# Attention and two feed-forward layers: the first 768 tokens in two phases, with g kept as float32 between the products

## The chip, the cores and the metric

The kernel runs on one core of a Trainium2 chip (trn2). Times are device microseconds of one execution, and the metric is their median over the runs. The engines are TensorE (PE, with its weight loads as PEld), VectorE (DVE), ScalarE (ACT), GpSimd (POOL, unused here) and SyncE (SP), which issues all DMA.

## What is computed

The reference, cut to what matters:

```python
# q, k, v: (4, 8, 576, 64)
scores = (1.0 / np.sqrt(D)) * np.matmul(q, k.transpose(0, 1, 3, 2))
mask = (rel >= 0) & (rel < 64)            # rel: query position minus key position
scores = np.where(mask, scores, -1000000000.0)
attn = softmax(scores)
x = np.matmul(attn, v)                    # heads side by side: (2304, 512)
x = np.maximum(x @ w_in, 0.0) ** 2 @ w_out      # first layer, 512 -> 2048 -> 512
h = x @ w_in2
out = np.maximum(0.01 * h, h) @ w_out2          # second layer
```

Inputs are float32. The host passes the weights as raw 64-bit words, and the kernel makes float32 of them.

## The kernel before

Every matmul of the two layers is done in three products of split operands: a float32 value is a high part (cast to fp32r by ScalarE, line 281) and a low part (the rest, a subtraction on VectorE, line 284), and high x high, high x low and low x high are added in PSUM. A weight chunk of 128 x 512 is first put together from its words: ScalarE scales one word (line 314), VectorE needs three passes (lines 317, 323, 329), and then it is split (lines 281 and 284). There are 16 chunks j of `w_in` and 16 of `w_out`. All 32 are converted once and stay in SBUF.

The 2304 tokens are 18 attention blocks of 128 queries. A block has two halves of four heads. The first four blocks go half by half (`quad`), later ones whole (`duo`): scores on TensorE (line 406) into bank s (and t or h), mask on VectorE (line 375), maximum (427), exponentials on ScalarE (430), sum and reciprocal (436, 437), normalisation (440), transposes (TensorE 463), a copy (ScalarE 281), weighing with the values (TensorE 472), and the split into x (`to_x`, ScalarE 281 and VectorE 284).

The first layer takes the tokens in `BLOCKS` of 512, 384, 512, 384, 512. For each chunk j, `step` computes the first product (line 571, 12 matmuls into a bank h), relu and square on ScalarE, the square again on VectorE (600) for the low part of g, and then the second product (line 617, 12 matmuls), which adds into four banks acc0 to acc3. The order on TensorE is first product of j+1, second product of j. In the first block of 512 tokens the first four chunks are cut into two waves of 256 tokens (`LAG`), since the second 256 tokens' x comes later. The result goes to DRAM as x2.

The second layer's weights are converted into DRAM meanwhile (`weight_to_dram`). The second layer (lines 801 and 890) works on 768 tokens at a time; its second product fills six banks in turn, three matmuls in each.

PSUM has eight banks: acc0 to acc3, two h, s and t. The order of work is not written by hand. Each operation is recorded with an engine, a cost and a due time (`op`), and `Plan.order` places them: a ready operation with the earliest due time goes first on its engine, and buffers are handed out in turn. Each engine then runs its list strictly in that order; SP issues the DMAs in its list in the same way.

Of the kernel before, what the change touches and what calls it, by code (L numbers as in the profile page):

```python
# [34 lines left out]
BLOCKS = [512, 384, 512, 384, 512]  # L35
# [214 lines left out]
def build(ctx, tc, qp, kp, vp, w1, w2, caps, ident, out, prm=PRM):  # L250
# [250 lines left out]
    def quad(i, b, c, e, sp_):  # L501
# [20 lines left out]
    def duo(b, e):  # L522
# [36 lines left out]
    def step(t, i, parts, T, dt, T2, busy, last):  # L559
        x = xt[t]  # L560
        nb = BLOCKS[t]
        hp = slot(ps_h, "h", [P, 512], F32, 2)
        c = slice(parts[0][0], parts[-1][0] + parts[-1][1])
        n = c.stop - c.start
# [3 lines left out]
        def ffn1(c0, n1, j, kk):
            wi = wt[j, 0].ap.rearrange("p v (k f) -> p v k f", k=KD)
            for m, (a, b) in enumerate(((0, 0), (0, 1), (1, 0))):  # L570
                nc.tensor.matmul(  # L571
                    out=hp.ap[:, c0 : c0 + n1], lhsT=wi[:, a, kk, :],
                    rhs=x.ap[:, b, kk, c0 : c0 + n1],
                    start=(kk == 0 and m == 0), stop=(kk == KD - 1 and m == 2),
                )

        for c0, n1, j in parts:
            w = wt[j, 0]
            for kk in range(KD):
                rd = [(x, m, kk, b) for m in range(2) for b in x_cols(t, c0, n1)]  # L580
                op(
                    "pe", 3 * mm_cost(n1), T, lambda a=(c0, n1, j, kk): ffn1(*a),
                    [(w, 0), (w, 1), *rd], [(hp, 0)],
                )
        op("pe", 0.0, T, lambda: None, [(hp, 0)], [("step", t, i)])
        hin = [(hp, 0)]
# [19 lines left out]

        if i == 0:
            acc[t] = [slot(ps_acc, f"acc{d}", [P, nb]) for d in range(KD)]
        ac = acc[t]

        def ffn2(d, ms):
            for m in ms:
                a, b = ((0, 0), (1, 0), (0, 1))[m]
                for c0, n1, j in parts:
                    wo = wt[j, 1].ap
                    begin, end = i == 0 and m == 0, last and m == 2
                    nc.tensor.matmul(  # L617
                        out=ac[d].ap[:, c0 : c0 + n1], lhsT=wo[:, a, d * P : (d + 1) * P],
                        rhs=g.ap[:, b, c0 : c0 + n1], start=begin, stop=end,
                        skip_group_check=True,  # L620
                    )
# [440 lines left out]
```

## Time and profile before

| | |
|---|---|
| median of 3 runs | 871.2 us (870.68 to 872.87) |
| the profiled execution, its own time | 871.45 us |
| its span in the trace | 869.7 us |
| busy: PE, PEld | 849.9 us (98%), 755.1 us (87%) |
| busy: DVE, ACT | 574.8 us (66%), 469.5 us (54%) |
| DMA | 103.59 MB, mean 119 GB/s |

Times inside the trace count from the start of the span. The profiled execution took 1.75 us more than its span, which lies before and after it. A matmul's record includes its way through the array, so the records of neighbours overlap; the distance from one group's start to the next is what a group costs. The same holds for VectorE, where one instruction's end overlaps the next one's start a little. A trace is one execution; the durations here come from it.

### The profile page before, as it was taken

What the parts mean: (1) busy time and instruction counts of PE and PEld (TensorE: products, weight loads), DVE (VectorE), ACT (ScalarE), POOL (GpSimd) and SP (SyncE); (2) the same over time, 40 slices, a digit from 0 to 9 for tenths busy, and PEclk for the clock granted to TensorE, in tenths of its full rate; (3) what the DMA queues carried; (4) which work ended last, traced back from release to release, by engine and by line L of the source; (5) the groups of instructions that cost most, each with busy time, mean ns of one, the idle gap of its engine ahead of it and who ended that gap; (6) DMA issues with size and microseconds to landing.
All of it is one profiled execution on the core that took longest, in us unless ns stands there. A gap on an engine that the chain in (4) does not pass through costs nothing.

```text
span 869.7 us, 13819 instructions
## 1 busy us (share of the span) xinstructions
PE 849.9 (98%) x5224; PEld 755.1 (87%) x5224; DVE 574.8 (66%) x1100; ACT 469.5 (54%) x1079; POOL 0.2 (0%) x4
## 2 busy tenths in 40 slices
PE   7879999999999999999999999999999999999998
PEld 6768887999888879999888899988999888999886
DVE  6989886555665577666768387775487774676530
ACT  4858676445453445444435377753477653667430
POOL 0000000000000000000000000000000000000000
PEclk8989999999999999999999999999999999999999
DMA  7554652223534436433543212431213422223201
GB/s 281 193 206 151 191 197 74 76 86 107 175 119 151 146 103 205 153 117 110 165 142 105 73 49 74 150 116 49 106 65 99 144 73 73 97 73 98 97 0 73
DMA packets 45570, 103.59 MB, mean 119 GB/s; under 512 B 5056, under 2 KB 6336, under 8 KB 45504
## 3 DMA queue, kind: packets, MB, share of 16 engines
q1 hardware_dynamic: 45504, 102.72, 35.2%
q8 instruction: 41, 0.67, 0.3%
q14 instruction: 25, 0.20, 0.1%
HBM read 84.87 MB, written 17.83 MB: 118 GB/s over the span
## 4 chain that ended last, share of the span: by engine, by line
PE 92%; DVE 4%; DMA 2%; ACT 2%; issue 0%; DVEq 0%; SPq 0%
PE acc L617 21%; PE h L571 21%; PE acc L890 15%; PE h L801 9%; PE s L801 6%; PE s L890 4%; PE t L890 4%; PE acc L801 3%; PE t L801 3%; PE t L472 2%; PE s L406 2%; PE t L463 2%; DMA wst<-w2a 1%; PE t L948 1%; DVE e L323 1%; DMA wst<-w1a 1%
## 5 line engine op out<-in xcount | busy, mean ns | idle before, releaser
L617 PE MATMUL acc<-g,w 128*128 128x512 f32 (+2 forms) x1008 | 220.7, 364 | 5.5 <-ACT g L281 4.2
L571 PE MATMUL h<-x,w 128*128 128x512 f32 (+2 forms) x1008 | 219.3, 363 | 3.5 <-DVE w L284 1.9
L617 PEld LDWEIGHTS acc<-g,w 128*128 128x128 f32 x1008 | 178.3, 190 | 27.9 <-ACT g L281 4.5
L571 PEld LDWEIGHTS h<-x,w 128*128 128x128 f32 x1008 | 177.4, 189 | 27.0 <-DVE w L284 2.7
L890 PE MATMUL acc<-w,w 128*128 128x512 f32 x576 | 146.2, 389 | 0.0
L890 PEld LDWEIGHTS acc<-w,w 128*128 128x128 f32 x576 | 108.1, 188 | 22.4
L284 DVE TENSOR_TENSOR w<-wst,w 128x512 fp32r<-128x512 f32 (+1 forms) x144 | 87.3, 642 | 30.0 <-ACT w L281 30.0
L591 ACT ACTIVATE e<-h 128x512 f32<-128x512 f32 (+2 forms) x84 | 45.0, 536 | 113.5 <-PE h L571 111.9
L281 ACT CAST w<-wst 128x512 fp32r<-128x512 f32 (+1 forms) x144 | 78.7, 582 | 44.0 <-PE acc L890 24.7
L801 PE MATMUL h<-w,w 128*128 128x384 f32 x432 | 85.1, 334 | 0.0
L600 DVE TENSOR_TENSOR e<-e 128x384 f32<-128x384 f32 (+1 forms) x64 | 39.9, 623 | 67.7 <-ACT g L599 67.7
L801 PEld LDWEIGHTS h<-w,w 128*128 128x128 f32 x432 | 75.9, 188 | 0.2
L284 DVE TENSOR_TENSOR g<-e,g 128x512 fp32r<-128x512 f32 (+2 forms) x84 | 51.6, 615 | 9.6 <-ACT g L281 4.7
L801 PE MATMUL s<-w,w 128*128 128x384 f32 x288 | 57.9, 335 | 0.0
L314 ACT ACTIVATE wst<-wst 128x512 f32<-128x512 f32 x64 | 42.5, 675 | 20.3 <-DMA wst<-w2b 11.2
L801 PEld LDWEIGHTS s<-w,w 128*128 128x128 f32 x288 | 50.7, 188 | 0.1
L323 DVE SCALAR_TENSOR_TENSOR e<-wst,e 128x512 int32<-128x512 int32 x64 | 44.3, 692 | 1.9
L329 DVE SCALAR_TENSOR_TENSOR e<-wst,e 128x512 int32<-128x512 int32 x64 | 44.2, 690 | 1.7
L640 DVE COPY e<-acc 128x512 f32<-128x512 f32 (+1 forms) x19 | 12.6, 664 | 49.3 <-PE acc L890 27.8
L890 PE MATMUL s<-w,w 128*128 128x512 f32 x144 | 40.5, 389 | 0.0
L890 PE MATMUL t<-w,w 128*128 128x512 f32 x144 | 40.4, 389 | 0.0
L284 DVE TENSOR_TENSOR w<-x,w 128x384 fp32r<-128x384 f32 x54 | 29.5, 553 | 13.9 <-ACT w L281 13.9
(129 smaller groups left out, 1005.5 us busy)
## 6 DMA issues: line engine op xcount, KB each, us to landing
wst<-wf SPq DMA_DIRECT2D x96, 256.0 KB, 2.9
wst<-w1a SPq DMA_DIRECT2D x16, 512.0 KB, 4.3
wst<-w2a SPq DMA_DIRECT2D x16, 512.0 KB, 3.7
v<-vp SPq DMA_DIRECT2D x32, 256.0 KB, 2.9
wst<-w1b SPq DMA_DIRECT2D x16, 512.0 KB, 4.5
wf<-e SPq DMA_DIRECT2D x32, 256.0 KB, 2.2
wst<-w2b SPq DMA_DIRECT2D x16, 512.0 KB, 4.3
w<-x SPq DMA_DIRECT2D x12, 384.0 KB, 4.0
```

The costliest lines, as they stand in the source:

```text
L281: nc.scalar.copy(out=dst, in_=src)
L284: eng.tensor_tensor(out=lo, in0=src, in1=f32(hi), op=ALU.subtract)
L314: nc.scalar.activation(out=top, in_=top, func=AF.Copy, scale=2.0**-112)
L323: nc.vector.scalar_tensor_tensor(out=cv.ap, in0=words(1), scalar=-(1 << 31), in1=cv.ap, op0=ALU.bitwise_and, op1=ALU.bitwise_or,)
L329: nc.vector.scalar_tensor_tensor(out=cv.ap, in0=words(0), scalar=29, in1=cv.ap, op0=ALU.logical_shift_right, op1=ALU.bitwise_or,)
L406: nc.tensor.matmul(out=st.ap[o : o + WIN, h, :], lhsT=q.ap[d, h, o : o + WIN], rhs=k.ap[d, h, o : o + P], start=True, stop=True,)
L571: nc.tensor.matmul(out=hp.ap[:, c0 : c0 + n1], lhsT=wi[:, a, kk, :], rhs=x.ap[:, b, kk, c0 : c0 + n1], start=(kk == 0 and m == 0), stop=(k ...
L591: nc.scalar.activation(out=r.ap, in_=hp.ap[:, c], func=AF.Relu)
L600: op("dve", dve_cost(n), a0 + 1.4, lambda: nc.vector.tensor_tensor(out=r.ap, in0=r.ap, in1=r.ap, op=ALU.mult), [], [(r, 0)])
L617: nc.tensor.matmul(out=ac[d].ap[:, c0 : c0 + n1], lhsT=wo[:, a, d * P : (d + 1) * P], rhs=g.ap[:, b, c0 : c0 + n1], start=begin, stop=end, ...
L801: nc.tensor.matmul(out=ps.ap, lhsT=view(v, i), rhs=xs[s, i][b].ap[:, u], start=begin and i == 0 and m == 0, stop=i == 1 and m == 2, skip_g ...
L890: nc.tensor.matmul(out=accs[3 * h + tt].ap, lhsT=v.ap[:, b, tt * P : (tt + 1) * P], rhs=w.ap[:, a, :], start=n == 0 and m == 0, stop=last ...
```

## The change

`BLOCKS` becomes 512, 256, 512, 512, 512, and the first two, 768 tokens, are done in two phases.

Phase one (`unit`) computes only first products. For chunk j, ScalarE writes relu of bank h as float32 into g and squares it in place; g of all 16 chunks stays in SBUF (16 tiles of 128 x 768: 14 in buffers of the tag w1, two in those of the tag g). The order is given by the list `first`: the first 256 tokens (A) for four chunks, the next 256 (BB) for the same four, all 512 (AB) for chunks 4 to 11, then the last 256 tokens (C) for chunks 0 to 11, then C and AB in turn for chunks 12 to 15. Only `w_in` is needed for that.

Phase two (`out_unit`) computes the second products. For each chunk, ScalarE casts g to its high part, VectorE subtracts for the low part, into one of two buffers `g_split`, which lie where x of the second block was. TensorE then does 12 matmuls of 256 columns (tokens 512 to 767) and 12 of 512 columns. The four accumulators of 512 columns have acc0 to acc3; the four of 256 columns share the two h banks, two in each, and the bank is opened by the first matmul of the first of them alone. The `w_out` chunks are converted for this phase, each into a buffer that an earlier g has left (`gate`).

The later blocks keep the old `step`, always with 512 tokens and without the form with an additional ScalarE pass that the first block had (`busy`). Transposes and weighing of the first six blocks use acc banks. Due times are new, and the second layer's g has one tile more in x1 and none in kl.

```diff
-BLOCKS = [512, 384, 512, 384, 512]
+BLOCKS = [512, 256, 512, 512, 512]
+NFIRST = 2
...
+NG = sum(BLOCKS[:NFIRST])
...
-    def weight(k, c):
+    def weight(k, c, gate=()):
...
-        op("act", act_cost(DM), c + 1.8 * cs, lambda: copy(w.ap[:, 0], f32(cv.ap)), [(cv, 0)], [(w, 0)])
+        op("act", act_cost(DM), c + 1.8 * cs, lambda: copy(w.ap[:, 0], f32(cv.ap)), [(cv, 0), *gate], [(w, 0)])
...
-        if early:
-            tp = slot(ps_acc, f"acc{i % 2 * 2}", [P, HQ, P])
-            pv = slot(ps_acc, f"acc{i % 2 * 2 + 1}", [P, HQ // 2, P])
-        else:
-            tp = slot(ps_t, "t", [P, HQ, P])
-            pv = slot(ps_t, "t", [P, HQ // 2, P])
+        tp = slot(ps_acc, f"acc{i % 2 * 2}", [P, HQ, P])
+        pv = slot(ps_acc, f"acc{i % 2 * 2 + 1}", [P, HQ // 2, P])
...
+    def ffn2(a, w, g, d, ms, first, last):
+        for m in ms:
+            i, b = ((0, 0), (1, 0), (0, 1))[m]
+            nc.tensor.matmul(
+                out=a, lhsT=w.ap[:, i, d * P : (d + 1) * P], rhs=g[:, b],
+                start=first and m == 0, stop=last and m == 2, skip_group_check=True,
+            )
...
+    def unit(t, c0, n, j, T, dt):
+
+        hp = slot(ps_h, "h", [P, n], F32, 2)
+        if j not in first_g:
+            own = (gp, "g", 2) if j >= NCH - 2 else (wp, "w1", NCH)
+            first_g[j] = slot(own[0], own[1], [P, NG], F32, own[2])
+        g = first_g[j]
...
+        ffn1(t, c0, n, j, hp, T)
...
+        op("act", act_cost(n), a0, lambda: nc.scalar.activation(out=part(), in_=hp.ap, func=AF.Relu), [(hp, 0)], keys)
+        op("act", act_cost(n), a0 + 0.7, lambda: nc.scalar.activation(out=part(), in_=part(), func=AF.Square), [], keys)
+
+    def out_unit(m, j, T, accs, gs_):
+
+        g, w, k = first_g[j], wt[j, 1], m % 2
+        for t in (1, 0):
...
+            op("act", act_cost(n), d0, lambda o=o, n=n, part=part: copy(part(0), g.ap[:, o : o + n]), src, [hi])
+            op("dve", dve_cost(n), d0 + 0.7, lambda o=o, n=n, part=part: sub(nc.vector, part(1), g.ap[:, o : o + n], part(0)), [hi, *src], [lo, ("split", m, t)])
+            one = mm_cost(n)
+            for d in range(KD):
+                a = accs[t][d]
+                shared = t == 1 and d % 2 == 1
...
+                    lambda d=d, a=a, o=o, n=n, shared=shared: ffn2(a[1](), w, gs_.ap[:, k, :, o : o + n], d, (0, 1, 2), m == 0 and not shared, m == NCH - 1),
...
+    units(A, range(LA), prm["PA"])
+    t_b = units(BB, range(LA), prm["PB"])
+    units(AB, range(LA, LB), prm["PAB"])
+    t_c = units(C, range(LB), prm["PC"])
+    for j in range(LB, NCH):
+        units(C, [j], 12 * mm_cost(HALF))
+        units(AB, [j], 12 * mm_cost(512))
...
+    g_split = slot(xp, "x1", [P, 2, 2, NG], F32R)
...
+    two = [slot(ps_h, "h", [P, 2, HALF], F32, 2) for _ in range(2)]
...
+    for m, j in enumerate(out_order):
+        weight(2 * j + 1, t_f + m * step1 - prm["LEAD2"], [("split", m - 2, t) for t in range(NFIRST)])
+        out_unit(m, j, t_f + m * step1, acc, g_split)
```

How the change moves instructions, at three places. VectorE in the kernel before, from one low part of x of block 3 to the next, its second half's. Line 317 begins a chunk's conversion, line 284 ends it; w_656 is of `w_in`, w_664 of `w_out`, and x_323 is x of the first 512 tokens:

```order
L284 TENSOR_TENSOR x_323<-t,x_323 128x2x128
L436 TENSOR_SCALAR sm<-sm 128x4
L437 RECIPROCAL rc<-sm 128x4
L440 TENSOR_TENSOR pt<-pt,rc 128x512
L284 TENSOR_TENSOR g<-e,g 128x256
L284 TENSOR_TENSOR w_656<-e,w_656 128x512
L284 TENSOR_TENSOR w_664<-e,w_664 128x512
L317 TENSOR_SCALAR e<-wst 128x512
L323 SCALAR_TENSOR_TENSOR e<-wst,e 128x512
L329 SCALAR_TENSOR_TENSOR e<-wst,e 128x512
L317 TENSOR_SCALAR e<-wst 128x512
L284 TENSOR_TENSOR x_323<-t,x_323 128x2x128
```

VectorE in the changed order, the last rows up to the same low part of x (here x_334; pt and u on lines 378 and 430 are block 4's, and w_591 is the fifth chunk of `w_in`):

```order
L439 TENSOR_SCALAR sm<-sm 128x4
L440 RECIPROCAL rc<-sm 128x4
L443 TENSOR_TENSOR pt<-pt,rc 128x512
L378 SCALAR_TENSOR_TENSOR u<-s,cap 64x512 x2
L430 TENSOR_REDUCE nm<-u 128x4
L287 TENSOR_TENSOR x_334<-acc_306,x_334 128x2x128
L287 TENSOR_TENSOR w_591<-e,w_591 128x512
L320 TENSOR_SCALAR e<-wst 128x512
L326 SCALAR_TENSOR_TENSOR e<-wst,e 128x512
L378 SCALAR_TENSOR_TENSOR pt<-t,cap 64x512 x2
L430 TENSOR_REDUCE nm<-pt 128x4
L287 TENSOR_TENSOR x_334<-acc_318,x_334 128x2x128
```

The low parts of g and the chunks of `w_out` are gone from the list ahead of this x, and block 4's masks and maxima now stand there.

TensorE in the changed order, where the units on the last 256 tokens begin (line 475 weighs block 5, x_334 is x of the first 512 tokens, x_810 of the last 256, w_316 and w_374 are chunks 0 and 1 of `w_in`):

```order
L606 MATMUL h<-x_334,w_910 128x512 x12
L466 MATMUL acc_306<-ident,pt 128x128 x4
L606 MATMUL h<-x_334,w_953 128x512 x9
L475 MATMUL acc_267<-u,v 64x64 x8
L475 MATMUL acc_267<-pt,v 64x64 x8
L606 MATMUL h<-x_334,w_953 128x512 x3
L606 MATMUL h<-x_810,w_316 128x256 x12
L606 MATMUL h<-x_810,w_374 128x256 x12
```

The three matmuls after the weighing are the rest of chunk 11's unit; the next row reads x_810, of which the weighing just made the last block.

TensorE in the kernel before, in the first 512 tokens (w_961 and w_1040 are of `w_in`, w_923 of `w_out`):

```order
L571 MATMUL h<-x_323,w_961 128x512 x12
L617 MATMUL acc_241<-g,w_923 128x512 x2
L617 MATMUL acc_298<-g,w_923 128x512 x2
L617 MATMUL acc_252<-g,w_923 128x512 x2
L617 MATMUL acc_313<-g,w_923 128x512 x2
L617 MATMUL acc_241<-g,w_923 128x512
L617 MATMUL acc_298<-g,w_923 128x512
L617 MATMUL acc_252<-g,w_923 128x512
L617 MATMUL acc_313<-g,w_923 128x512
L571 MATMUL h<-x_323,w_1040 128x512 x12
```

TensorE in the changed order, at the start of phase two (x_1396 is `g_split`, w_1107 the last chunk of `w_in`, w_1161 and w_1179 the first two of `w_out`):

```order
L606 MATMUL h<-x_810,w_1107 128x256 x12
L606 MATMUL h<-x_334,w_1107 128x512 x12
L618 MATMUL h<-x_1396,w_1161 128x256 x6
L618 MATMUL acc_238<-x_1396,w_1161 128x512 x3
L618 MATMUL h<-x_1396,w_1161 128x256 x6
L618 MATMUL acc_306<-x_1396,w_1161 128x512 x3
L618 MATMUL acc_267<-x_1396,w_1161 128x512 x3
L618 MATMUL acc_318<-x_1396,w_1161 128x512 x3
L618 MATMUL h<-x_1396,w_1179 128x256 x12
L618 MATMUL acc_238<-x_1396,w_1179 128x512 x3
```

Where first and second products alternated, all second products of these tokens now follow all first ones, and the h banks hold accumulators.

## Rows read from the trace of the kernel before

**Rows 1.** The page, parts 1 and 2: busy time, and busy tenths in 40 slices.
```profile
PE 849.9 (98%) x5224; PEld 755.1 (87%) x5224; DVE 574.8 (66%) x1100; ACT 469.5 (54%) x1079; POOL 0.2 (0%) x4
...
PE   7879999999999999999999999999999999999998
```

**Rows 2.** Windows: start:end, length, busy of PE, PEld, DVE, ACT, POOL, clock, DMA, GB/s.
```profile
20.00:40.00 20.00, 16.06 (x173) 14.03 (x172) 19.62 (x42) 16.09 (x43) 0.00 (x0) 0.90 0.59 199
40.00:60.00 20.00, 13.51 (x128) 12.06 (x126) 16.68 (x35) 12.90 (x38) 0.00 (x0) 0.83 0.48 170
...
200.00:300.00 100.00, 100.00 (x670) 85.63 (x670) 60.59 (x109) 44.39 (x109) 0.00 (x0) 1.00 0.42 142
553.00:865.00 312.00, 312.00 (x1535) 278.44 (x1534) 192.24 (x383) 169.40 (x338) 0.00 (x0) 1.00 0.25 82
```

**Rows 3.** Critical chain from 60 to 90 us: start us, us, what.
```profile
61.33 2.79 PE h L571 x21
...
67.46 1.44 PE h L571 x12
...
77.27 2.72 PE acc L617 x12
...
84.10 1.13 PE t L472 x32
```

**Rows 4.** VectorE groups by line and form, 0 to 140 us: count | busy us, mean ns.
```profile
L323 DVE SCALAR_TENSOR_TENSOR e<-wst,e 128x512 int32<-128x512 int32 x32 | 22.1, 691 | 0.8
...
L284 DVE TENSOR_TENSOR w<-e,w 128x512 fp32r<-128x512 f32 x31 | 21.0, 686 | 1.8 <-ACT w L281 1.4
L317 DVE TENSOR_SCALAR e<-wst 128x512 int32<-128x512 int32 x32 | 13.5, 421 | 0.4 <-ACT wst L314 0.3
...
L440 DVE TENSOR_TENSOR pt<-pt,rc 128x512 f32<-128x512 f32 x5 | 3.5, 691 | 0.1
...
L427 DVE TENSOR_REDUCE nm<-u 128x4 f32<-128x512 f32 x5 | 3.4, 682 | 0.1
...
L284 DVE TENSOR_TENSOR g<-e,g 128x256 fp32r<-128x256 f32 x8 | 3.4, 419 | 0.0
...
L437 DVE RECIPROCAL rc<-sm 128x4 f32<-128x4 f32 x14 | 2.5, 178 | 0.5
L436 DVE TENSOR_SCALAR sm<-sm 128x4 f32<-128x4 f32 x14 | 2.3, 162 | 0.0
```

**Rows 5.** VectorE in order of time: start us, us, instruction [idle before <-releaser].
```profile
8.06 1.39 DVE L375 SCALAR_TENSOR_TENSOR w<-s,cap 64x512 f32<-64x512 f32 x2 [7.07 <-PE s L406]
...
59.75 0.42 DVE L284 TENSOR_TENSOR x<-t,x 128x256 fp32r<-128x256 f32 x1 [2.21 <-ACT x L281]
```

**Rows 6.** TensorE in order of time: the scores of one block and what follows them.
```profile
309.39 0.33 PE L406 MATMUL s<-kh,qs 64*64 64x128 f32 x2
...
310.42 3.06 PE L571 MATMUL h<-x,w 128*128 128x512 f32 x12
```

**Rows 7.** TensorE groups by line and form, 0 to 61.25 us.
```profile
L571 PE MATMUL h<-x,w 128*128 128x256 f32 x60 | 10.1, 307 | 2.7 <-DVE x L284 1.5 <-DVE w L284 1.1
L617 PE MATMUL acc<-g,w 128*128 128x256 f32 x48 | 9.1, 329 | 5.5 <-ACT g L281 4.2 <-DVE g L284 1.3
```

**Rows 8.** VectorE in order of time: a low part of x.
```profile
86.36 0.69 DVE L284 TENSOR_TENSOR x<-t,x 128x512 fp32r<-128x512 f32 x1
```

**Rows 9.** ScalarE groups by line and form, 0 to 140 us.
```profile
L430 ACT ACTIVATE pt<-pt,nm 128x128 f32<-128x128 f32 x20 | 7.8, 392 | 0.0
...
L281 ACT CAST g<-e 128x256 fp32r<-128x256 f32 x8 | 3.2, 406 | 0.2
...
L430 ACT ACTIVATION_READ_ACCUMULATOR pt<-pt,nm 128x1 f32 x20 | 3.8, 189 | 0.0
```

**Rows 10.** SP's waits, 0 to 150 us: who for whom: total, times, longest.
```profile
SPq L497 <- PE t L472: 34.7, 5, 15.7
```

**Rows 11.** Critical chain from 0 to 140 us.
```profile
44.19 5.45 DMA wst<-w1a
```

More of the change, by code (lines that the diff above doesn't have):

```diff
@@ L557, in x_cols, with step @@
         return range(o // P, (o + n) // P)
-    def step(t, i, parts, T, dt, T2, busy, last):
+    def step(t, j, T, dt, T2, last):
         x = xt[t]
[L561 to L564, printed above, removed]
+        n = BLOCKS[t]
+        hp = slot(ps_h, "h", [P, n], F32, 2)
         r = slot(ep, "e", [P, n])
         g = slot(gp, "g", [P, 2, 512], F32R, 2)
[L568 to L586, printed above, removed]
+        ffn1(t, 0, n, j, hp, T)
+        op("pe", 0.0, T, lambda: None, [(hp, 0)], [("step", t, j)])
         a0 = T + dt + 0.1
@@ L605, in step @@
         )
[L607 to L621, printed above, removed]
@@ L623, in step, with out @@
-        one = sum(mm_cost(p[1]) for p in parts)
-        ws = [wt[p[2], 1] for p in parts]
-        wh, wl = [(w, 0) for w in ws], [(w, 1) for w in ws]
+        if j == 0:
+            acc[t] = [slot(ps_acc, f"acc{d}", [P, n]) for d in range(KD)]
+        w = wt[j, 1]
+        one = mm_cost(n)
+        def out(d, ms):
+            return lambda: ffn2(acc[t][d].ap, w, g.ap[:, :, 0:n], d, ms, j == 0, last)
         if not last:
             for d in range(KD):
-                op("pe", 2 * one, T2, lambda d=d: ffn2(d, (0, 1)), [gh, *wh, *wl], [(ac[d], 0)])
+                op("pe", 2 * one, T2, out(d, (0, 1)), [gh, (w, 0), (w, 1)], [(acc[t][d], 0)])
@@ L960, in build @@
         pair_load(b, e - early - 6.0 if b < prm["NDUO"] else e + gap - prm["DS"] - 6.0)
-    for k in range(2 * NCH):
-        st = next(q for q in steps if q[2][0][2] == k // 2)
-        weight(k, st[3] + (k % 2) * st[4] - prm["LEAD"])
+    for j in range(NCH):
+        weight(2 * j, next(u[4] for u in first if u[3] == j) - prm["LEAD"])
+    new_x(0)
+    new_x(1)
+    g_split = slot(xp, "x1", [P, 2, 2, NG], F32R)
     for i, (e, b, c, gap) in enumerate(quads):
@@ L968, in build @@
             duo(b, e)
-    for n, (t, i, parts, T, dt, wave) in enumerate(steps):
-        last = n + 1 == len(steps) or steps[n + 1][0] != t
-        T2 = steps[n + 1][3] + steps[n + 1][4] if n + 1 < len(steps) else t_end
-        step(t, i, parts, T, dt, T2, wave, last)
+    for n, (t, c0, nb, j, T) in enumerate(first):
+        unit(t, c0, nb, j, T, 12 * mm_cost(nb))
+    accs = {0: [slot(ps_acc, f"acc{d}", [P, 512]) for d in range(KD)]}
+    two = [slot(ps_h, "h", [P, 2, HALF], F32, 2) for _ in range(2)]
@@ new lines, in build, with store @@
+    for t in range(NFIRST):
+        acc[t] = []
+        for d in range(KD):
+            if t == 0:
+                acc[t].append(((accs[0][d], 0), lambda a=accs[0][d]: a.ap))
+            else:
+                acc[t].append(((two[d // 2], d % 2), lambda a=two[d // 2], d=d: a.ap[:, d % 2, :]))
+    for m, j in enumerate(out_order):
+        weight(2 * j + 1, t_f + m * step1 - prm["LEAD2"], [("split", m - 2, t) for t in range(NFIRST)])
+        out_unit(m, j, t_f + m * step1, acc, g_split)
+    def store(t, a, d, due):
+        o, nb = starts[t], BLOCKS[t]
+        evac(a, nb, x2[d][:, o : o + nb], [(("x2", d, t), 0)], d % 2 == 0, due)
@@ L973, in build @@
+    for t in (1, 0):
+        for d in range(KD):
+            store(t, acc[t][d], d, t_start[NFIRST] - 12 * mm_cost(512) * t + prm["EV0"] + prm["EV1"] * (d + 1) / KD)
+    for n, (t, j, T, dt) in enumerate(steps):
+        last = j == NCH - 1
+        T2 = steps[n + 1][2] + steps[n + 1][3] if n + 1 < len(steps) else t_end
+        step(t, j, T, dt, T2, last)
         if last:
-            o, nb = starts[t], BLOCKS[t]
             for d in range(KD):
-                due = T2 + prm["EV0"] + prm["EV1"] * (d + 1) / KD
-                evac(acc[t][d], nb, x2[d][:, o : o + nb], [(("x2", d, t), 0)], d % 2 == 0, due)
+                a = acc[t][d]
+                store(t, ((a, 0), lambda a=a: a.ap), d, T2 + prm["EV0"] + prm["EV1"] * (d + 1) / KD)
```

122 lines of the change are left out of this document (78 added, 44 removed).

## The prediction

> **What bounds the kernel now.** I read the page first, for the slices by engine [rows 1], then the busy time by stretch [rows 2], TensorE's chain in order of time [rows 3], and VectorE's instructions by group [rows 4]. The slices say that TensorE is full almost throughout: 849.9 of 869.7 us, the digits 9 from the fourth slice (65 us) on. So time can be won only before that, or by giving TensorE less work. The stretches say why it isn't full early: VectorE is busy 19.62 of the 20 us from 20 to 40 and 16.68 from 40 to 60, while TensorE is busy 16.06 and 13.51, at a granted clock of 0.90 and 0.83 [rows 2]. A fraction means time at both levels, 1.2 and 2.4 GHz; later stretches have 1.00, all at the upper one.
>
> What ends the poor stretch is one operation: VectorE writes the low part of x for the second half of block 3, the last of the first 512 tokens, from 59.75 to 60.17 us [rows 5]. At 61.33 us TensorE starts first products of the second 256 columns and runs on [rows 3]. Up to there VectorE feeds both products: each chunk of `w_in` and each of `w_out` costs it one L317, one L323, one L329 and one L284.
>
> **The change, term by term.** I work out when that operation comes now, and how much TensorE work is left behind it in each kernel.
>
> *VectorE up to that operation.* In the order of the kernel before there stand up to it 12 L317, 22 of L323 and L329, 10 low parts of weights, 4 of g, 10 masks, 8 maxima, 8 pairs of sum and reciprocal, 8 normalisations and 8 low parts of x. With the means of [rows 4], a mask counted like a normalisation and a low part of x like one of g: 12 x 0.42 + 22 x 0.69 + 10 x 0.69 + 4 x 0.42 + 10 x 0.69 + 8 x 0.68 + 8 x 0.34 + 8 x 0.69 + 8 x 0.42 = 52.7 us. From the first mask at 8.06 us that gives 60.8; the trace has 60.17 [rows 5]. So the method is 0.6 us off: neighbouring instructions overlap a little, and that pays for the waits. In the changed order there stand 6 L317, 11 of L323 and L329, 5 low parts of weights, none of g, 14 masks and 10 maxima (block 4's come earlier), and the same 8, 8 and 8: 2.5 + 7.6 + 3.5 + 9.7 + 6.8 + 2.7 + 5.5 + 3.4 = 41.7 us. From 8.06 us that is **49.7 us**, 11.6 us before the 61.33 at which TensorE ran on. Just ahead on TensorE's queue stand the scores of block 5; the second of their banks comes free with a mask that ends 1.1 us before that operation, at 48.6, and scores take 1.03 us, from 309.39 to 310.42 [rows 6]. So they end at the same time and cost nothing.
>
> *Work left at that point.* Before, 60 first-product and 48 second-product matmuls of 256 columns had run [rows 7]. After, by its order: the same 60, no second-product one, and the scores of block 5 besides those of block 4. Twelve matmuls of 256 columns take 1.44 us, twelve of 512 take 2.72 [rows 3]. So 48 x 0.12 = 5.8 us more is left, less 1.03 for the scores. The whole program has 48 second-product matmuls fewer (960 for 1008, the same columns): two of 256 cost 0.240 us where one of 512 costs 0.227, so this saves 48 x 0.013 = 0.6 us. 5.8 - 1.0 - 0.6 = **4.1 us** more.
>
> *New waits behind it.* The next transposes need a normalisation that stands 1.7 us down VectorE's list, and TensorE asks after 1.44 us: **0.3 us**. The seven chunks of w_in for the units of 512 columns that are not ready yet stand 5.2, 5.9, 10.2, 13.4, 17.3, 21.5 and 23.9 us down that list, by the same means; TensorE asks for them after 7.9, 11.8, 14.5, 17.2, 21.0, 24.1 and 27.3 us. The least cover is 2.6 us; beyond it each late us costs one. Then come twelve units of 256 columns on blocks 4 and 5. They need x of block 5, whose weighing stands only three matmuls of 512 columns (0.7 us) ahead of them. From the end of a weighing (85.23) to the end of such a low part (87.05) is 1.8 us [rows 3, 8]: TensorE waits **1.1 us**.
>
> *Phase two.* TensorE has 16 x (1.44 + 2.72) = 66.6 us, and 11.1 us of attention. VectorE's list (32 low parts of g, 14 of weights, 10 L317, 20 of L323 and L329, three blocks of softmax, four x) comes to 64 us, 82% of that: not the bound. The first split waits for the buffer of x of tokens 512 to 767, free 2.72 us before phase two; ScalarE's cast (0.41) and VectorE's subtraction (0.42) of 256 columns fit [rows 4, 9]. Later splits have more than a unit of 4.16 us. I take 0 for these, and for ScalarE's casts and copies, which run under the same cover. A pair of accumulators in one bank is not in the trace: its matmul is bounded below by the 0.12 us of 256 columns in a bank of their own and above by the 0.227 of 512. It writes 256 columns, so I take 0.12; the upper end would be 192 x 0.107 = 20 us. Transposes that go to the free acc banks add no instruction.
>
> *DMA.* No bytes are added. On SP's queue the `w_out` loads move behind all of `w_in`, and 13 of them ahead of the values of block 7, which can be loaded only after block 6 is weighed. SP stood 15.7 us at one load of values for TensorE's weighing [rows 10]; such waits stay, but only half the weight loads are queued behind them. I take nothing; the cover is the three staging buffers, and if it goes, the chunk's conversion is late and eats the 2.6 us above.
>
> *Later blocks of 512.* TensorE's columns are the same, and VectorE is busy 60.59 of 100 us there [rows 2]: nothing.
>
> **Sum.** 11.6 - 4.1 - 0.3 - 1.1 = 6.1 us. The profiled execution took 871.45 us (span 869.7), 0.25 above the median of 871.2. 871.45 - 6.1 = **865.3 us**. A measurement of this kernel can tell about 0.3%, 2.6 us, from no change.
>
> **The rivals.**
> - *The phase-two loop starves TensorE (slower).* One mechanism: a split may start only when TensorE has left its buffer two units ago, and on VectorE it stands between masks, maxima and normalisations that wait for ScalarE's exponentials (four of 0.39 + 0.19 us per half block [rows 9]). It has 5.6 us (a unit and 1.44) to 6.9 (a unit and 2.72). One block's rows with two splits among them fill 6.6 us even without waits; where the waits push a split past its 5.6 to 6.9 us, this decides. Then TensorE gaps, and its clock falls as from 20 to 40 us: 77.7 us at 0.90 instead of 1.00 is 8.6 us more, and 1.5 us a block for three blocks 4.5. That gives 873.9 to 878.4. For it: second-product matmuls waited 4.2 us for ScalarE's part of g early on [rows 7]. Against: VectorE has 18% spare. Chance 0.07.
> - *Rounds over six banks lower the clock.* Phase two issues three to six matmuls a bank and goes on to the next of six. If each change of bank idles TensorE briefly and the clock falls to 0.90 for that alone, the price is the 8.6 us: 873.9. Against it: line 890 goes round six banks with three matmuls each, and the stretch that it shares with line 801 is busy 312.00 of 312 us at 1.00 [rows 2]. Chance 0.02. The Trainium skill ("TensorE: Matmul & The Clock Gate", section "A second HAM failure mode: psum-queue depth-cycling") says that cycling through PSUM banks each iteration can idle TensorE often enough between groups that its clock goes up and down. By that rule this rival would be the likely case; the trace does not agree for line 890.
> - *The saving goes to another wait (no change).* The chain has 5.45 us of a w_in load from 44.19 us [rows 11], and VectorE itself was free 3.3 us between 40 and 60: it was not alone. If loads or exponentials hold it in phase one for 4 to 6 us beyond what the method paid for, x comes at 54 to 56 us: 869 to 871. Against: half the weight loads and all of g's low parts are gone from there. That the second weights aren't put off at all would end here too; the order excludes it. Chance 0.20.
> - *VectorE runs without waits (faster).* Up to 60.17 us it was idle 3.2 us (the largest 2.21 [rows 5]), so its busy time was 48.9 us, 0.93 of 52.7. 41.7 x 0.93 brings x at 46.8 us, 2.9 earlier, and with the two waits (1.4 us) gone: 861.0. Against: TensorE's own queue then ends later than x. Chance 0.12.
>
> **The numbers.** My forecast has 0.59, spread from 862.5 to 868.7. With the fast rival and a quarter of the no-change rival, faster by over 0.3% (under 868.6) has 0.75; the rest of that rival, a part of the banks' and the forecast's upper edge give 0.17 within 0.3%; slower (over 873.8) has 0.08. The range goes from the fast rival's 861 to 871, the end of the no-change rival; it leaves out the slow ones and a part of the fast.
>
> **What would show it.** Right: the low part of x for the second half of block 3 ends near 49.7 us; from there TensorE is busy over 19.5 of every 20 us at a clock of 1.00, with a gap of about 1 us before the first unit on blocks 4 and 5, near 80 us; phase two begins near 116 us and ends near 194; the tail is unchanged. Wrong: x near 55 us; or gaps between 116 and 194 us that end with splits, and a clock below 1.00; or twelve matmuls into shared banks at more than 1.44 us.

## The result, and the profile after

The changed kernel takes **864.06 us** (median of 4 runs, 861.98 to 864.92), the kernel before took 871.63 beside it. The ratio is 0.9909, 95% interval 0.9887 to 0.9931. The forecast was 865.3. The profiled execution took 864.92 us, with a span of 862.8 against 869.7.

The page of the changed kernel, its parts 1 and 2:

```profile
PE 849.9 (99%) x5176; PEld 738.3 (86%) x5176; DVE 568.2 (66%) x1080; ACT 471.4 (55%) x1091; POOL 0.2 (0%) x4
...
PE   8899999999999999999999999999999999999998
```

TensorE's busy time is 849.9 us as before [rows 1]. (The equal totals hide two things: there are 48 matmuls fewer, and more of the early work ran at the lower clock, 0.75 from 20 to 40 us for 0.90 before.) So the 6.9 us by which the span shrank are idle time of TensorE, 19.8 us before and 12.9 after. The stretches show where (columns as in [rows 2]):

```profile
20.00:40.00 20.00, 18.37 (x213) 15.86 (x211) 17.70 (x39) 15.75 (x54) 0.00 (x0) 0.75 0.52 165
40.00:60.00 20.00, 17.37 (x155) 15.34 (x155) 17.21 (x35) 15.86 (x44) 0.00 (x0) 0.91 0.56 195
60.00:80.00 20.00, 20.00 (x146) 16.13 (x145) 15.72 (x30) 16.02 (x40) 0.00 (x0) 1.00 0.59 191
80.00:100.00 20.00, 19.44 (x174) 18.21 (x173) 18.02 (x32) 17.24 (x39) 0.00 (x0) 1.00 0.66 207
...
120.00:220.00 100.00, 100.00 (x774) 85.24 (x775) 72.29 (x136) 53.23 (x141) 0.00 (x0) 1.00 0.37 122
```

From 20 to 60 us TensorE is busy 35.7 us, against 29.6 [rows 2]. The low part of x for the second half of block 3, which came at 59.75 to 60.17 [rows 5], in VectorE's order of time:

```profile
48.54 0.69 DVE L430 TENSOR_REDUCE nm<-pt 128x4 f32<-128x512 f32 x1
49.26 0.42 DVE L287 TENSOR_TENSOR x<-acc,x 128x256 fp32r<-128x256 f32 x1
```

It ends at 49.68 us. TensorE's order of time, from the last scores ahead of the second 256 columns, through the gap before the units on blocks 4 and 5, to both ends of phase two (line 618):

```profile
49.90 0.63 PE L409 MATMUL t<-kh,qs 64*64 64x128 f32 x4
50.46 1.75 PE L606 MATMUL h<-x,w 128*128 128x256 f32 x12
52.05 0.60 PE L466 MATMUL acc<-ident,u 128*128 128x128 f32 x4
...
83.58 34.41 PE L606 MATMUL h<-x,w 128*128 128x256 f32 x239 [0.55 <-DVE x L287]
...
117.83 0.88 PE L618 MATMUL h<-x,w 128*128 128x256 f32 x6
...
122.01 1.60 PE L618 MATMUL h<-x,w 128*128 128x256 f32 x12
123.45 2.91 PE L618 MATMUL acc<-x,w 128*128 128x512 f32 x12
126.19 1.60 PE L618 MATMUL h<-x,w 128*128 128x256 f32 x12
...
194.52 2.91 PE L618 MATMUL acc<-x,w 128*128 128x512 f32 x12
197.27 5.60 PE L606 MATMUL h<-x,w 128*128 128x512 f32 x24
```

In the same view of the kernel before, the second 256 columns go on at 61.26 us (the chain in [rows 3] counts the same start as 61.33), and there is one more wait, which I hadn't counted and which is gone:

```profile
61.26 2.85 PE L571 MATMUL h<-x,w 128*128 128x256 f32 x21
...
137.78 1.20 PE L571 MATMUL h<-x,w 128*128 128x512 f32 x4 [0.80 <-DVE w L284]
```

So TensorE goes on 10.8 us earlier, at 50.46. The span shrank by 6.9 us, so 3.9 were given back. The windows from that point to the end show how, first of the changed kernel, then of the kernel before:

```profile
50.46:862.80 812.34, 807.67 (x4726) 701.71 (x4724) 528.68 (x999) 438.58 (x978) 0.00 (x0) 1.00 0.34 113
```

```profile
61.26:869.70 808.44, 803.51 (x4758) 714.58 (x4756) 525.64 (x1000) 430.49 (x962) 0.00 (x0) 1.00 0.34 111
```

TensorE is busy 4.16 us longer behind that point, and idle 4.67 us instead of 4.93: the new gap of 0.55 at 83.58 came, the wait of 0.80 went. The 4.16 us are the second products that are now done behind that point, less the scores of block 5, which now stand ahead of it, and less what the 48 matmuls fewer save.

### The profile page after: what moved, and what is told of

It is laid out like the page before. It is cut to its first block, busy times and chain, and to the rows that moved or that the text cites. A ratio compares the mean times of both kernels' runs of the same rounds, so it can differ in the third digit from the quotient of the medians.

```text
span 862.8 us, 13690 instructions
## 1 busy us (share of the span) xinstructions
PE 849.9 (99%) x5176; PEld 738.3 (86%) x5176; DVE 568.2 (66%) x1080; ACT 471.4 (55%) x1091; POOL 0.2 (0%) x4
## 4 chain that ended last, share of the span: by engine, by line
PE 95%; DVE 3%; ACT 1%; DMA 1%; issue 0%; DVEq 0%
PE h L606 23%; PE acc L618 20%; PE acc L918 15%; PE h L829 9%; PE s L829 6%; PE s L918 4%; PE t L918 4%; PE acc L829 3%; PE t L829 3%; PE h L618 3%; PE s L409 2%; PE t L475 2%; PE t L466 1%; PE t L991 1%; PE acc L466 1%; PE acc L475 0%
## 5 line engine op out<-in xcount | busy, mean ns | idle before, releaser
L606 PE MATMUL h<-x,w 128*128 128x512 f32 (+1 forms) x1008 | 215.9, 366 | 2.3 <-DVE x L287 2.2
L606 PEld LDWEIGHTS h<-x,w 128*128 128x128 f32 x1008 | 169.4, 191 | 32.9 <-DVE x L287 2.6
L618 PE MATMUL acc<-g,w 128*128 128x512 f32 x576 | 141.4, 392 | 0.0
L618 PEld LDWEIGHTS acc<-g,w 128*128 128x128 f32 x576 | 107.3, 188 | 22.0
L577 DVE TENSOR_TENSOR e<-e 128x512 f32<-128x512 f32 x48 | 33.1, 691 | 50.9 <-ACT g L576 50.7
L572 ACT ACTIVATE e<-h 128x512 f32<-128x512 f32 x48 | 28.5, 593 | 48.9 <-PE h L606 48.9
L618 PE MATMUL acc<-x,w 128*128 128x512 f32 x192 | 48.2, 395 | 0.0
L433 ACT ACTIVATE u<-u,nm 128x128 f32<-128x128 f32 x64 | 25.0, 395 | 34.5 <-DVE nm L430 34.5
L287 DVE TENSOR_TENSOR w<-x,w 128x384 fp32r<-128x384 f32 x60 | 32.6, 554 | 12.4 <-ACT w L284 12.4
```

Of the source, the lines that this page charges most:

```text
L287: eng.tensor_tensor(out=lo, in0=src, in1=f32(hi), op=ALU.subtract)
L433: nc.scalar.activation(out=u.ap[:, h, :], in_=u.ap[:, h, :], func=AF.Exp, bias=nm.ap[:, h : h + 1], scale=1.0, accum_out=sm.ap[:, h : h + 1],)
L572: nc.scalar.activation(out=r.ap, in_=hp.ap, func=AF.Relu)
L606: nc.tensor.matmul(out=hp.ap, lhsT=wi[:, a, kk, :], rhs=x.ap[:, b, kk, c0 : c0 + n], start=(kk == 0 and m == 0), stop=(kk == KD - 1 and m ...
L618: nc.tensor.matmul(out=a, lhsT=w.ap[:, i, d * P : (d + 1) * P], rhs=g[:, b], start=first and m == 0, stop=last and m == 2, skip_group_chec ...
```

## The experiments

Theory A is that of the prediction: VectorE's list ahead of x of block 3 sets the early stretch, and the time follows it nearly one to one. Each run was timed beside the kernel before (its medians lie between 871.70 and 872.03). "By the rows' means", in the expectations, is the sum of means along VectorE's order, as in the prediction.

**1. VectorE's work put back.**

```diff
-        op("dve", dve_fast(DM), c, conv0, [(raw, 0)], [(cv, 0)])
...
+        for _ in range(again):
+            op("dve", dve_fast(DM), c, conv0, [(raw, 0)], [(cv, 0)])
...
+        again = 2 if k < 12 and k % 2 == 0 else 1
...
```

The two other passes and the subtraction of the low part are repeated in the same way.

> VectorE does the three conversion passes and the low part of the first six chunks of w_in twice (the second time with the same result), so roughly the VectorE work that the postponed w_out chunks took is put back ahead of the x of block 3; loads, ScalarE and TensorE are unchanged. Theory A (VectorE's list sets the end of the early stretch, and the time follows it): by the means of the rows the low part of x for the second half of block 3 comes at 58.3 us instead of 49.7, 8.6 later, TensorE goes on near 59, and the time is 864.1 + 8.6 = 872.7 (870.5 to 875). Theory B (the gain is from the block sizes, the order of TensorE's work or the saved loads, and VectorE has room): under 867, whatever x does.

Measured: 872.85 us, ratio to before 1.0015 (1.0006 to 1.0023): the whole gain is gone, with the order, the blocks and the loads of the changed kernel. VectorE and TensorE in order of time:

```profile
56.15 0.42 DVE L287 TENSOR_TENSOR x<-acc,x 128x256 fp32r<-128x256 f32 x1
```

```profile
56.47 7.58 PE L609 MATMUL h<-x,w 128*128 128x256 f32 x48
...
66.14 1.89 PE L609 MATMUL h<-x,w 128*128 128x512 f32 x7 [1.20 <-DVE w L287]
...
125.60 0.88 PE L621 MATMUL h<-x,w 128*128 128x256 f32 x6
```

x came 6.9 us later, not 8.6, and TensorE waited 1.20 more for a chunk whose doubled conversion was late; phase two began 7.8 later. Theory B falls.

**2. The blocks alone.** In the kernel before:

```diff
-BLOCKS = [512, 384, 512, 384, 512]
+BLOCKS = [512, 256, 512, 512, 512]
...
```

> The kernel before with only the blocks changed to 512, 256, 512, 512, 512 (and the buffers that g takes over from x cut accordingly); first and second product alternate as before. Theory A: VectorE's list up to the low part of x for the second half of block 3 is unchanged (by the rows' means 61.9 us as in the kernel before), TensorE goes on near 61, and the time is that of the kernel before, 871.6 (869.5 to 873.5). Theory B (block sizes carry the gain): 868 or less.

Measured: 870.58 us, ratio 0.9991 (0.9981 to 1.0000). The block sizes alone carry at most 0.2%.

**3. VectorE relieved in the old order.** First with GpSimd, in the kernel before:

```diff
+        on_pool = k < 11
+        eng = nc.gpsimd if on_pool else nc.vector
         op(
-            "dve", dve_cost(DM), c + 2.5 * cs,
+            "pool" if on_pool else "dve", 1.4 if on_pool else dve_cost(DM), c + 2.5 * cs,
-            lambda: sub(nc.vector, w.ap[:, 1], f32(cv.ap), w.ap[:, 0]),
+            lambda: sub(eng, w.ap[:, 1], f32(cv.ap), w.ap[:, 0]),
```

> The kernel before, its order and blocks untouched, with the low part of its first eleven weight chunks (six of w_in, five of w_out) subtracted on GpSimd. It takes VectorE work away ahead of x of block 3 without the two phases: by the rows' means that x stands at 53.9 us in VectorE's list instead of 61.9, 8 less. Theory A in its strong form (the time follows VectorE's list in either order): 863.5 to 866. Theory H (in the old order the t bank, ScalarE's casts of g and TensorE's second products hold x too, so that the two phases are needed for the gain): 867 to 871.

Measured: 872.95 us, ratio 1.0009 (0.9996 to 1.0022). Neither theory had this. GpSimd's order of time, and VectorE's beside it:

```profile
21.25 1.27 POOL L284 TENSOR_TENSOR w<-e,w 128x512 fp32r<-128x512 f32 x1 [20.81 <-ACT w L281]
25.59 1.28 POOL L284 TENSOR_TENSOR w<-e,w 128x512 fp32r<-128x512 f32 x1 [3.06 <-ACT w L281]
29.87 1.43 POOL L284 TENSOR_TENSOR w<-e,w 128x512 fp32r<-128x512 f32 x1 [3.00 <-ACT w L281]
```

```profile
21.45 1.63 DVE L442 TENSOR_TENSOR w<-w,rc 128x512 f32<-128x512 f32 x1
...
25.45 0.67 DVE L429 TENSOR_REDUCE nm<-pt 128x4 f32<-128x512 f32 x1
26.14 1.01 DVE L317 TENSOR_SCALAR e<-wst 128x512 int32<-128x512 int32 x1
...
30.08 1.50 DVE L317 TENSOR_SCALAR e<-wst 128x512 int32<-128x512 int32 x1
```

A normalisation that takes 0.69 us alone took 1.63, and line 317 took 1.01 and 1.50 instead of 0.42, where a subtraction on GpSimd had begun just before them. Ten instructions were 8.4 us longer in all; 11 x 0.69 = 7.6 us had been moved. So VectorE was not relieved, and x came at 60.29. That makes the run no test of theory A. The next one leaves work out instead, again in the kernel before:

```diff
-    def float_words(s, j, m, c, cv, after=()):
+    def float_words(s, j, m, c, cv, after=(), sign=True):
...
-        op("dve", dve_cost(DM), c + 0.4 * cs, conv1, [(raw, 0)], [(cv, 0)])
+        if sign:
+            op("dve", dve_cost(DM), c + 0.4 * cs, conv1, [(raw, 0)], [(cv, 0)])
...
-        float_words(0, j, m, c, cv)
+        float_words(0, j, m, c, cv, sign=not (k < 11))
```

> The kernel before, order and blocks untouched; the second conversion pass (line 323, which carries the sign bit over) is left out for the first eleven weight chunks, so those weights lose their sign. In the run with GpSimd VectorE was not relieved at all: ten of its instructions that met a subtraction on GpSimd took 8.4 us longer than their like, as much as the 7.6 us that were moved. Here nothing takes its place. By the rows' means x of block 3 stands at 52.5 us in VectorE's list instead of 61.9. Theory A (the time follows VectorE's list in the old order too): 863 to 866. Theory H (the one t bank, ScalarE's casts of g and the second products behind them hold x): 867 to 871.

Measured: **862.45 us**, ratio 0.9893 (0.9877 to 0.9908): as much as the whole change brings, and a little more than theory A's range, with old order, old blocks and alternating products. VectorE's order of time, then TensorE's:

```profile
52.18 0.42 DVE L284 TENSOR_TENSOR x<-t,x 128x256 fp32r<-128x256 f32 x1
```

```profile
54.25 3.15 PE L572 MATMUL h<-x,w 128*128 128x256 f32 x24
```

x is 7.6 us earlier and TensorE goes on 7.0 earlier; its profiled execution (863.72) is 7.7 us shorter. Nothing is given back here, since no work was put off: behind that point TensorE is busy 803.29 us, against 803.51 in the kernel before. Theory H falls.

One thing this run doesn't part. VectorE's passes also set when a load's staging buffer comes free; SP's waits in the kernel before, 0 to 150 us:

```profile
SPq L305 <- DVE e L329: 58.4, 23, 5.6
```

The chain of the kernel before has a load of 5.45 us at 44.19 [rows 11], and the low part of x itself waited 2.21 us for ScalarE [rows 5]; the chain of this run has no load up to 54 us. So "VectorE's list" stands for VectorE's time together with the loads that hang on it.

**4. The accumulator banks for transposes and weighing.** In the changed kernel, blocks 2 to 5 go through the t bank again:

```diff
-        tp = slot(ps_acc, f"acc{i % 2 * 2}", [P, HQ, P])
-        pv = slot(ps_acc, f"acc{i % 2 * 2 + 1}", [P, HQ // 2, P])
+        if early:
+            tp = slot(ps_acc, f"acc{i % 2 * 2}", [P, HQ, P])
+            pv = slot(ps_acc, f"acc{i % 2 * 2 + 1}", [P, HQ // 2, P])
+        else:
+            tp = slot(ps_t, "t", [P, HQ, P])
+            pv = slot(ps_t, "t", [P, HQ // 2, P])
...
-        free = b < sum(BLOCKS[:NFIRST]) // P
+        free = False
```

> The changed kernel, but the transposes and the weighing of blocks 2 to 5 go through the one t bank again instead of the free accumulator banks. Theory A: fewer banks push the weighings back, and x of block 3 stands later in VectorE's list, by the rows' means at 52.3 instead of 49.7 us: 2.7 later, 866.7 us (865.5 to 868). Theory B (the banks carry much of the gain, as each weighing has to wait for the bank): 869 or more. Theory C (the bank was free in time anyway): 864.1 within 1.

Measured: 870.02 us, ratio 0.9984 (0.9975 to 0.9994): 6.0 us more than the changed kernel, theory B. x of block 3 ended at 51.42, only 1.74 later. Its profiled execution was the longest of 12 (872.91), so its waits are an upper end. In the order of time, SP, ScalarE and TensorE:

```profile
84.91 0.80 SPq L500 DMA_DIRECT2D v<-vp  x2
```

```profile
96.82 0.66 ACT L317 ACTIVATE wst<-wst 128x512 f32<-128x512 f32 x1 [3.00 <-DMA wst<-w2a]
97.38 0.37 ACT L642 ACTIVATE w<-h 128x256 f32<-128x256 f32 x1
```

```profile
97.80 22.56 PE L610 MATMUL h<-x,w 128*128 128x256 f32 x148 [2.28 <-ACT w L642]
```

The chain of the same run has the load for which ScalarE waited:

```profile
89.47 7.33 DMA wst<-w2a
```

SP stood 6.4 us, until 84.91, at the values of block 6, for the weighing of block 5 (84.15 to 85.36). The loads behind them then followed one another. The `w_out` load at 89.47, which had waited 0.4 us more for VectorE to free its buffer, took 7.33 us to land, where such loads take 3.8 in the changed kernel (the median). ScalarE waited 3.00 us for it, with the relu of a unit queued behind, and TensorE waited 2.28 for that relu. That the stand of SP made this load slow is argued from the order of the loads, not shown by a run of its own.

Half of the edit, blocks 2 and 3 alone in the t bank (the first part of the diff above):

> Half of the t-bank experiment: only blocks 2 and 3 transpose and weigh in the t bank again, blocks 4 and 5 keep the free accumulator banks. If the 6.0 us that it cost came from x of block 3 being later (1.74 us in its trace), 866 (865 to 867). If most came from here through other waits, 868 or more.

Measured: 869.05 us, ratio 0.9970 (0.9959 to 0.9981): most of the 6.0 us is here, and again not through x, which ended at 50.50. TensorE's order of time in the profiled execution (867.49, the shortest of 11):

```profile
49.57 0.43 PE L409 MATMUL s<-kr,qr 64*64 64x128 f32 x4
50.56 0.33 PE L409 MATMUL t<-kr,qr 64*64 64x128 f32 x2 [0.56 <-DVE x L287]
...
51.58 4.84 PE L610 MATMUL h<-x,w 128*128 128x256 f32 x36
56.35 0.33 PE L409 MATMUL s<-kh,qs 64*64 64x128 f32 x2
...
57.39 2.34 PE L610 MATMUL h<-x,w 128*128 128x512 f32 x9
...
92.04 28.33 PE L610 MATMUL h<-x,w 128*128 128x256 f32 x190 [1.00 <-ACT w L642]
```

The scores of block 4 need the t bank and wait until x has been read out of it; those of block 5 run at 56.35. In the changed kernel both lie ahead of 50.46 (37.34 and 48.31), where TensorE would otherwise have waited for VectorE. Here TensorE goes on 1.12 us later, has another 1.04 us of scores behind that point, and waits 1.00 instead of 0.55: 2.6 us together, as its execution is 2.57 us longer than the profiled one of the changed kernel. The medians are further apart (5.0 us), and one trace each does not show what the longer runs add.

**5. Is VectorE still the bound in the changed kernel?** Three runs. The low parts of five `w_in` chunks on GpSimd (as in 3, with k < 10 and even):

> The changed kernel, but the low part of the first five chunks of w_in is subtracted on GpSimd, which is idle in the trace (0.2 us of 862.8). By the rows' means that takes x of block 3 from 49.7 to 43.8 us in VectorE's list. Theory A as long as VectorE alone sets the stretch: up to 5.9 us less, 858 to 861. Theory D (from there TensorE's own queue, at the low clock that it has between 20 and 50 us, or ScalarE's exponentials bound it): 862 to 865. No row shows what a subtraction of 128x512 costs on GpSimd, or whether it slows VectorE; if it takes over 2 us, the weights are late for TensorE, and the time is above 865.

Measured: 861.90 us, ratio 0.9886 (0.9873 to 0.9898). x came at 46.56. Here three VectorE instructions beside a subtraction on GpSimd were 2.1 us longer than their like, 1.1 of that ahead of x. The same pass left out as in 3, for six `w_in` chunks (they lose their sign):

> The changed kernel with the same pass left out for the first six chunks of w_in (they lose their sign): x of block 3 stands at 45.1 us in VectorE's list instead of 49.7. Theory A (VectorE's list still sets the stretch in the changed kernel): 859.5 to 861. Theory D (TensorE's stretch at half clock, the chain of scores, masks, exponentials and transposes, or ScalarE do): 862 to 863.7.

Measured: 860.87 us, ratio 0.9880 (0.9862 to 0.9898), theory A. x came at 46.10, 3.6 us earlier, and the median is 3.2 us under the changed kernel's. And TensorE's clock, by fourteen more idle matmuls ahead of the poor stretch:

```diff
-    SPARE=0.2, NACT=0, WARM=20, WC=0.3, WD=1e6, AL=0.6, CS=0.7,
+    SPARE=0.2, NACT=0, WARM=34, WC=0.3, WD=1e6, AL=0.6, CS=0.7,
```

> The changed kernel with 34 instead of 20 of the idle 128x128 matmuls of line 991 (they write a bank that nobody reads), so that the fourteen more lie in TensorE's gaps between 11 and 17 us, ahead of the stretch from 17 to 31 us in which TensorE was busy at a granted clock of 0.50. Theory A (VectorE's list sets x of block 3, and VectorE waits only 2.5 us before it): at most 1 us for x and 0.75 for the scores that ran at the low clock just ahead of it: 862.5 to 863.7. Theory E (the low clock is what costs: 11 to 13 us of TensorE's work at half speed): 859 to 861. If the additional matmuls stand in the way, 864.5 or more.

Measured: 863.11 us (862.99 to 863.20), ratio 0.9900 (0.9885 to 0.9914), theory A. Windows of the changed kernel, then of this one (columns as in [rows 2]):

```profile
12.00:16.00 4.00, 1.72 (x20) 1.27 (x20) 3.87 (x8) 3.97 (x18) 0.00 (x0) 1.00 1.04 398
18.00:30.00 12.00, 11.67 (x105) 9.88 (x104) 11.51 (x26) 8.21 (x27) 0.00 (x0) 0.50 0.49 153
...
47.00:50.00 3.00, 3.00 (x37) 2.78 (x38) 2.91 (x6) 2.00 (x7) 0.00 (x0) 0.53 0.31 93
```

```profile
12.00:16.00 4.00, 3.29 (x34) 2.58 (x33) 3.87 (x9) 4.00 (x20) 0.00 (x0) 1.00 1.04 401
18.00:30.00 12.00, 9.35 (x116) 8.27 (x114) 11.65 (x29) 8.06 (x27) 0.00 (x0) 0.86 0.49 156
...
47.00:50.00 3.00, 2.71 (x44) 2.37 (x40) 2.87 (x7) 1.97 (x9) 0.00 (x0) 1.00 0.43 102
```

After a stretch with 1.72 of 4 us busy, the clock was 0.50 from 18 to 30 us (1.2 GHz throughout), and TensorE was busy 11.67 of 12 us, which looks like the bound. With the clock at 0.86 TensorE is busy only 9.35 us, yet x came at 48.59, only 1.1 us earlier, and the median falls by 0.95 us, which is less than the 2.9 us over which the changed kernel's four runs lie. VectorE, busy 11.5 and 11.65 of 12 us in the two, sets the pace.

Both together, GpSimd and matmuls:

> The same fourteen matmuls, with five low parts of weights on GpSimd as well. There x of block 3 came at 46.6 us, while VectorE's list gives 43.8, and TensorE had 0.50 until 26 us. If TensorE's early clock held x back in that kernel, x comes at 44 to 45 us, and the time is 1 to 2.5 us under that kernel's 861.9: 859.4 to 860.9. If ScalarE's exponentials and loads held it, 861.9 within 0.7.

Measured: **861.08 us** (860.93 to 861.51), ratio 0.9877 (0.9864 to 0.9890), the fastest of the kernels that leave no work out. x came at 45.81, between the two expectations. Then, with both of these kept, the softmax of block 3 in slots of its own:

```diff
...
-        u = slot(wp, "w1", [P, HQ, P], F32, NCH) if early else slot(ap, ("u", "pt")[i % 2], [P, HQ, P])
+        if early or b == 3:
+            u = slot(wp, "w1" if early else "w0", [P, HQ, P], F32, NCH)
+        else:
+            u = slot(ap, ("u", "pt")[i % 2], [P, HQ, P])
```

> Low parts of weights on GpSimd and the fourteen additional matmuls as before, and besides this the softmax of block 3 in two free slots of w_in instead of the two buffers of block 2, so that VectorE's masks no longer wait for TensorE's weighing (1.46, 0.77 and the like in the trace of that kernel, 3.7 us of idle VectorE in all). If these waits still bound the stretch: 1 to 2.5 us under 861.1, that is 858.6 to 860.1. If not (by the rows' means x of block 3 stands at 45.1 us of VectorE's list, where it came at 45.8 before): 861.1 within 0.7.

Measured: 863.95 us, ratio 0.9917 (0.9901 to 0.9933), outside both expectations: 2.9 us slower than without. With the buffers free, the planner put block 3's first mask and the scores of block 4 further ahead, and VectorE waited 3.25 us for ScalarE's part of x later; x came at 49.74.

**6. The phase-two loop.** One `g_split` buffer instead of two:

```diff
-        g, w, k = first_g[j], wt[j, 1], m % 2
+        g, w, k = first_g[j], wt[j, 1], 0
...
-        weight(2 * j + 1, t_f + m * step1 - prm["LEAD2"], [("split", m - 2, t) for t in range(NFIRST)])
+        weight(2 * j + 1, t_f + m * step1 - prm["LEAD2"], [("split", m - 1, t) for t in range(NFIRST)])
```

The second part makes the conversion of a `w_out` chunk wait for the split of the chunk just before it, not of the one before that, so the run changes two things.

> The changed kernel with one buffer for the split g instead of two, so that a split of the next chunk waits until TensorE has left that part of this chunk: 2.7 us of cover for the 256 columns and 1.4 us for the 512, against 5.6 and 6.9. Cast and subtraction of 512 columns take 0.6 + 0.7 us and stand between other work on ScalarE and VectorE. Theory F (the loop is near its limit, as the slow rival of the prediction had it): TensorE waits 0.5 to 1 us at each of 15 chunks, 872 to 880. Theory G (ScalarE and VectorE take up a split at once): under 0.15 us a chunk, 864 to 866.

Measured: 866.56 us, ratio 0.9941 (0.9928 to 0.9954): 2.5 us more than with two, nearer to theory G and half a microsecond over its range. TensorE's order of time, with the three longest waits, and its window:

```profile
142.75 2.57 PE L618 MATMUL acc<-x,w 128*128 128x512 f32 x10 [0.48 <-DVE x L287]
152.40 0.73 PE L475 MATMUL t<-u,v 128*64 128x64 f32 x16 [0.27 <-ACT pt L284]
164.25 2.57 PE L618 MATMUL acc<-x,w 128*128 128x512 f32 x10 [0.37 <-DVE x L287]
```

```profile
120.00:200.00 80.00, 78.42 (x621) 65.71 (x620) 60.03 (x112) 44.36 (x114) 0.00 (x0) 1.00 0.35 109
```

Without the second buffer TensorE idles 1.58 us in 80, with it 0.00 of 100, and the clock stays at 1.00. The profiled execution (866.50) is 1.58 us longer than that of the changed kernel. Of the waits above two are for splits, one is for the attention, and none is for a `w_out` chunk.

## Why the prediction was right, and where it was off

- *What bounds the kernel.* Right, and shown from three sides: VectorE's work put back takes all of the gain (1), taken away in the old order gives all of it (3), and taken away once more in the new order gives 3.2 us more (5). The loads that wait for VectorE move along with its work in 3; in 1 the chain up to x has no load in it, and VectorE is its largest part.
- *VectorE up to that operation.* 49.7 us was forecast, 49.68 came. The method of means along the list, as the prediction counts it, held for both kernels within 0.6 us. In the experiments with GpSimd idle it was up to 1.7 us off (58.3 for 56.57 in 1). The expectations of 2 and 3 put the kernel before at 61.9, where the prediction has 60.8 and the trace 60.17; so the 9.4 us less that they give for the run without the pass were 7.6. And the method is blind to what GpSimd does to VectorE.
- *TensorE goes on at 49.7.* It did at 50.46. "They end at the same time and cost nothing" failed: the scores of block 5 took from 48.31 to 50.46 instead of 1.03 us, since the clock was 0.53 there. In the run with more matmuls that stretch has 1.00.
- *Work left.* 4.1 us forecast, 4.2 by the windows above.
- *New waits.* The 0.3 us at the next transposes didn't come: they stand right behind their matmuls at 52.05, since TensorE had come there 0.8 us later than forecast. The gap before blocks 4 and 5 was 0.55, not 1.1; the stretch with it, 80 to 100 us, is busy 19.44 of 20 us, just under the 19.5 that the prediction named. The 0.80 of the kernel before at 137.78 us was missing from my sum, on the good side. So the sum is near partly because its misses cancel: 0.8 us too much gain by the start, 0.3, 0.55 and 0.8 too little by the waits.
- *Phase two.* It lasted 79.4 us, not 77.7: 16 x (1.44 + 2.74) = 66.9, so the attention in it took 12.5 and not 11.1. It started at 117.83 and not near 116. Neither cost time, since TensorE had no gap in it. Twelve matmuls into shared banks took 1.44 us (122.01 to 123.45), the lower bound, as taken.
- *Transposes in the free banks "add no instruction".* True, but this step had no price, and taking it back costs 5 to 6 us (4), of which the trace with blocks 2 and 3 there accounts for 2.6. The sum did not suffer, I think because the order that I counted along held the move already: block 4's masks stood ahead of x in it, and the scores of blocks 4 and 5 lay in TensorE's gaps.
- *DMA.* "I take nothing" held: from 0 to 150 us SP waited 13.2 us for TensorE's weighing, at most 4.1 at one load, where it had waited 34.7 and up to 15.7 [rows 10]. From 60 to 110 us it waited 1.2; without the banks it was 10.7 there, and in that run ScalarE and TensorE waited for a load.
- *The rivals.* The saving did not go to another wait: x came at 49.68, not at 54 to 56. The phase-two loop did not starve TensorE; even with one buffer of the two it costs 2.5 us (6), where that rival stood 8.6 to 13.1 us above the forecast. The six-bank rounds left the clock at 1.00 with 100 of 100 us busy, so the rule of the Trainium skill ("TensorE: Matmul & The Clock Gate", section "A second HAM failure mode: psum-queue depth-cycling") is not borne out at three to six matmuls a bank. The fast rival's limit was right in kind: TensorE was 0.8 us behind x.

Against the median the sum is 1.2 us too high, against the profiled execution 0.4.

## What to carry to other kernels

Where one engine's list sets an early stretch, add up that list to the operation that releases the main engine, and count what was put off behind it: here both agreed with the traces within 0.6 us. It doesn't take two phases to win this: 7.6 us of passes left out of that list in the old order won as much (862.45 us), while the same amount moved to GpSimd won nothing. A bank that lets independent work run in the main engine's gaps can be worth a large part of such a gain (5 to 6 us here), though it adds and removes no instruction.

## What I had not expected of the hardware

GpSimd and VectorE get in each other's way. A subtraction of 128x512 took 1.27 to 1.81 us on GpSimd (its spans in a trace are rough), and VectorE instructions that began during it ran up to 1.1 us longer; a maximum that ran beside one (25.45 to 26.12 us) did not. The Trainium skill ("SBUF — State Buffer", section "Who interferes with whom") states that the two share a port pair as an exclusive lock, which VectorE's instructions with two SBUF inputs, or in a 2-port mode, contend for and a reduction doesn't. The rows agree for the normalisation, whose two inputs lie in SBUF, and for the maximum; the mode of line 317 no row names.
The early clock may also make the spread: the changed kernel's four runs lie 2.9 us apart, the four with fourteen more idle matmuls 0.2 us, and from 18 to 30 us the trace of the one has 0.50, that of the other 0.86. One trace each doesn't show it for the single runs, but every run's mean granted clock is on record. Of 29 runs of the kernel before, the 13 at 0.992 have a mean of 871.0 us and the 9 at 0.988 one of 872.5; in experiment 2 the six at 0.991 or 0.992 lie between 869.6 and 870.6 us, the five at 0.987 between 871.2 and 872.4. So part of the spread goes with the clock; that the clock causes it, no run shows.
